# A fused gated-memory attention and MLP kernel on one core: a new hand-written issue order, with the last rows of w_in loaded behind q and k of steps 0 and 1

## The chip, the cores and the metric

The kernel runs on one NeuronCore of a Trainium2 chip. TensorE (PE) multiplies matrices into PSUM; VectorE (DVE), ScalarE (ACT) and GpSimd (POOL) work on what PE leaves there and on SBUF; SyncE (SP) issues all transfers from and to the chip's memory. Every engine takes its own instructions strictly in the order in which the program lists them and waits where one needs another engine's result. The metric is the time of one execution on the device in microseconds (us), median over runs; less is better.

## The reference

Two parts follow each other. The first is a recurrent attention with gates, for 4 batches and 8 heads over 768 positions with head size 40; the second is a two-layer MLP over the 3072 rows that it gives.

```python
for t in range(S):
    m_new = np.maximum(f_gate[:, :, t] + m, i_gate[:, :, t])
    f_stab = np.exp(f_gate[:, :, t] + m - m_new)
    i_stab = np.exp(i_gate[:, :, t] - m_new)
    m = m_new
    C = f_stab[..., None, None] * C + i_stab[..., None, None] * np.einsum('bhd,bhe->bhde', vt, kt)
    n = f_stab[..., None] * n + i_stab[..., None] * kt
    h_tilde = np.einsum('bhde,bhe->bhd', C, qt)
    denom = np.maximum(np.abs(np.einsum('bhd,bhd->bh', n, qt)[..., None]), 1.0)
    y[:, :, t] = o * h_tilde / denom          # o = sigmoid(o_gate)
x = y.transpose(0, 2, 1, 3).reshape(B * S, H * D)         # 3072 x 320
h = x @ w_in                                              # 320 x 2048
g = h * erf(np.maximum(h, 0.0) + np.log1p(np.exp(-np.abs(h))))
return g @ w_out                                          # 2048 x 320
```

## The kernel before, in words

**Attention.** The 768 positions are cut into 6 chunks of 128; with 4 batches that makes 24 steps s = 4c + b. `gate_chunk(c)` (line 369) scans the gates of a chunk for all batches at once (tokens gload, scan, sum, rest, split, at, atc, and cumw and decw, which write the running sums to DRAM to be read back in a broadcast form). `attention(s)` (line 446) does one step: load brings q and k (512 KB), loadv brings k, v and the output gate (484 KB); for the first four steps the decay matrix comes from PE (pe, two halves, lines 527 to 530) and ACT (ex), later from a broadcast read (bq), an add on POOL (add) and ex; sel masks it on POOL; S multiplies k and q (line 604, and 617 and 623 from chunk 1 on); w multiplies by the decay on DVE; ph gives the step's output (711, 718, 724); ab, rc, cl, yg, y and yy divide and gate it; tr (791) transposes it on PE; xh and xl split it into a rounded part and the rest for the MLP.

**Weights.** w_in and w_out are split likewise. w_in comes in four column parts p and two blocks k of 128 rows (`weights_in`, line 878, token win with p and k: win00, win01, win10, ...; 512 KB each), and its last 64 rows in two transfers of 256 KB to the two halves of the partitions (`weights_tail`, line 889, tokens tail0 for parts 0 and 1, tail1 for parts 2 and 3). val (ACT), dec (DVE), hi and lo decode them; for win00 to win11 the rest comes by PE (lp, lines 860 and 861). For the tail the tokens are valt, dect, hit and lot.

**MLP.** `mlp(f)` (line 980) is one of 24 phases. A phase has two halves g = 0, 1. In each, two up tokens (line 1031) multiply x by w_in into two PSUM banks, hb copies each bank to SBUF (ACT or DVE), sp (softplus) and er (erf) run on ACT, each with a table switch (line 258) unless the table stands, mu multiplies on DVE (1065), gh rounds (ACT or DVE), gl takes the rest (1076, DVE or POOL), and two dn tokens multiply by w_out (1111 to 1114). up f.0 and f.1 with dn f.0 and f.1 are the first half, up f.2 and f.3 with dn f.2 and f.3 the second. The first two phases keep g whole and have no gh and gl. o copies the sums out and st stores them.

**Order.** Nothing is scheduled when the program is built. `SEQUENCE` (line 155) is a list of tokens written by a search outside the kernel; `Plan.issue` (line 68) calls the parts in this order, so it is the program order of every engine's instructions and of SP's transfers:

```python
        for token in sequence:
            if token[0] == '+':
                for _ in range(int(token[1:])):
                    self.filler.fn()
            else:
                name, _, k = token.partition('.')
                found[name][int(k or 0)].fn()
```

A token +n issues n filler matmuls (line 333), which multiply constants into a bank that nobody reads; the token fill is one more. `ENGINES` (line 92) says for parts that two or three engines can do which one does them. `HOMES` (line 130) says for every buffer, in the order of issue, which place it gets: big are the 4 KB places in SBUF, bank six banks of PSUM, letters a to f. A new tile in a place waits until all readers of the old one are done.

In the list of before, S of step 1 stands ahead of S of step 0, and SP's transfers begin gload0, cst, win01, win10, gload1, loadv0, tail0, load1, loadv1, load0, load2, gload2, win00, loadv2.

Of the kernel before, what the change touches and what calls it, by code (L numbers as in the profile page):

```python
# [93 lines left out]
hb0.0 hb0.3 hb1.0 hb1.1 hb1.2 hb1.3 hb10.0 hb10.1 hb10.2 hb10.3 hb11.0 hb11.2 hb11.3 hb12.0 hb12.1 hb12.2  # L94
hb12.3 hb13.0 hb13.1 hb13.2 hb13.3 hb14.2 hb14.3 hb15.0 hb15.1 hb15.2 hb16.0 hb16.1 hb16.2 hb16.3 hb17.0
hb17.2 hb18.3 hb19.0 hb19.1 hb19.2 hb19.3 hb2.0 hb2.1 hb2.2 hb2.3 hb20.0 hb20.1 hb20.3 hb21.0 hb21.1 hb21.3
hb22.0 hb22.3 hb23.2 hb23.3 hb3.0 hb3.1 hb3.3 hb4.0 hb4.2 hb4.3 hb5.1 hb5.3 hb6.1 hb6.2 hb6.3 hb7.1 hb7.3
hb8.1 hb8.3 hb9.0 hb9.2 sk0.0 sk1.0 sk3.0
# [67 lines left out]
wout8 sel4 dn0.1 hio4 hio0 load5 dq4 ma4 bq7 dq5 valo8 hb1.3 hii21 deco8 sp1.1 wout6 ma5 hb1.0 hb1.1 sp1.0 er1.0
S5 w5.0 vg4 S4 mk4 na4 bq6 qa5 dn0.0 dn0.2 dq7 hio2 mk5 loi21 w4.1 w4.0 cumw2 qa4 add7 tail1 dn0.3 er1.1 ph4 na5
w5.1 ph5 mu1.0 win20 wout9 valo6 deco6 mu1.1 dq6 yg5 add6 o0.0 ab4 o0.1 th4 yg4 hio3 loo3 hio8 load6 ab5 loadv6
rc5 ma7 hio6 gexp2 loo6 loo8 dn1.0 cl5 valt1 load7 win31 rc4 decw2 cl4 y4 yy4 ex7 y5 rest3 ex6 dn1.1 dn1.3 yy5
dect1 hio1 tr4 valo9 deco9 xh4 xl4 at3 atc3 win30 tr5 xh5 xl5 hit3 dn1.2 loadv7 hit2 hio9 lpo9 nk4 nk5 bq8 up2.0  # L170
# [15 lines left out]
ab11 rc11 gl6.0 cl11 load13 y11 dn5.3 o5.1 up7.2 load14 dn6.1 ma12 w12.1 mk12 qa12.1 yy11 tr11 xh9 xl9 sp6.1
xh11 sp7.0 add13 dq13 hb7.2 xl11 xl10 ex13 sel13 dn6.0 ma13 up7.3 vg13 qa12.0 th12 up9.0 er6.1 mu6.1 gh6.1 hb7.3
hb9.0 th13 bq15 qz13 S13 ph12 ab12 w13.0 mk13 er7.0 mu7.0 rc12 cl12 gl6.1 rest4 cumw4 sp7.1 er7.1 add15 ex15
na13 na12 gh7.0 nk12 dq15 up9.2 w13.1 up8.2 qa13.0 add14 mu7.1 dn6.2 st4.0 yg12 y12 yy12 dn6.3 gexp4 loadv15
up10.2 dq14 hb8.2 nk13 hb9.2 gh7.1 up8.3 ex14 gl7.0 tr12 xh12 xl12 up8.0 th15 loadv14 dn7.1 qa13.1 sel15 th14  # L190
vz15 up10.0 gload5 qz14 scan5 hb10.2 ph13 sum5 hb8.0 qa14.1 sel14 vg14 load15 vz14 ma14 dn7.0 rest5 loadv17
gl7.1 S14 hb10.0 up10.1 qa14.0 w14.0 mk14 na14 nk14 up8.1 ab13 hb8.3 hb10.1 vg15 qz15 qa15.1 vz16 at5 w14.1 ma15
S15 dn7.2 atc5 mk15 up9.3 ph14 w15.1 rc13 cl13 sp8.1 hb8.1 yg13 qz19 qa15.0 w15.0 ph15 y13 hb9.3 sp8.0 yy13 tr13
er8.1 ab14 rc14 up10.3 na15 ab15 rc15 er8.0 at4 sp9.1 yg15 cl15 y15 decw4 o7.0 hb10.3 mu8.0 gh8.0 xh13 yy15
# [1025 lines left out]
```

## Time and profile before

| | us |
|---|---|
| median of 3 runs | 444.38 |
| the runs | 444.38, 444.69, 440.9 |
| the profiled execution | 444.52 |
| its span, from the first to the last instruction | 442.8 |
| PE busy in it | 435.2 |

The span is 1.7 us shorter than the time of the same execution. Times in rows count from the start of the span. In a row of the timeline a piece of neighbouring instructions is shown together, with the count behind the x; since matmuls overlap, the time from the start of one piece to the start of the next is what it costs PE. A waiting time in square brackets names who ended it.

### The profile page before, as it was taken

What the parts mean: (1) busy time and instruction counts of PE and PEld (TensorE: products, weight loads), DVE (VectorE), ACT (ScalarE), POOL (GpSimd) and SP (SyncE); (2) the same over time, 40 slices, a digit from 0 to 9 for tenths busy, and PEclk for the clock granted to TensorE, in tenths of its full rate; (3) what the DMA queues carried; (4) which work ended last, traced back from release to release, by engine and by line L of the source; (5) the groups of instructions that cost most, each with busy time, mean ns of one, the idle gap of its engine ahead of it and who ended that gap; (6) DMA issues with size and microseconds to landing.
All of it is one profiled execution on the core that took longest, in us unless ns stands there. A gap on an engine that the chain in (4) does not pass through costs nothing.

```text
span 442.8 us, 12907 instructions
## 1 busy us (share of the span) xinstructions
PE 435.2 (98%) x5404; PEld 386.2 (87%) x5404; DVE 328.4 (74%) x588; ACT 326.2 (74%) x423; POOL 171.9 (39%) x175
## 2 busy tenths in 40 slices
PE   8899999999999999999999999999999999999996
...
PEclk9789999999999999999999999999999999999999
...
GB/s 201 329 306 291 164 173 350 99 185 94 181 231 122 127 145 48 172 130 92 121 33 151 178 152 46 83 166 119 114 89 4 3 0 1 0 31 0 46 1 59
DMA packets 31373, 53.52 MB, mean 121 GB/s; under 512 B 4308, under 2 KB 19444, under 8 KB 31316
## 3 DMA queue, kind: packets, MB, share of 16 engines
q1 hardware_dynamic: 31316, 52.71, 39.1%
...
## 4 chain that ended last, share of the span: by engine, by line
PE 65%; DVE 1%; issue 1%; ACT 0%; ACTq 0%
PE h L1031 29%; PE po L1111 10%; PE po L1114 10%; PE po L1112 10%; PE pa L711 2%; PE pa L617 2%; PE pa L791 1%; PE pa L623 1%; DVE st L682 0%; DVE st L689 0%; DVE z L647 0%; DVE gl L1076 0%; DVE o L1124 0%; ACT o L279 0%; DVE z L633 0%
## 5 line engine op out<-in xcount | busy, mean ns | idle before, releaser
L1031 PE MATMUL h<-xx,wh 128*128 128x256 f32 (+1 forms) x768 | 180.7, 340 | 1.4 <-issue 1.2
L1031 PEld LDWEIGHTS h<-xx,wh 128*128 128x128 f32 x768 | 125.6, 188 | 16.2 <-issue 0.5
L1111 PE MATMUL po<-woh,gh 128*128 128x320 f32 x352 | 106.8, 312 | 0.0
L1112 PE MATMUL po<-wol,gh 128*128 128x320 f32 x352 | 105.5, 309 | 0.0
L258 ACT ACT_TABLE_LOAD x80 | 102.6, 1283 | 1.5
L1031 PE MATMUL h<-xx,wl 128*128 128x256 f32 (+1 forms) x256 | 86.3, 337 | 0.0
L1065 DVE TENSOR_TENSOR hb<-e,hb 128x1024 f32<-128x1024 f32 x44 | 57.6, 1321 | 36.9 <-ACT e L1057 36.7
L1114 PE MATMUL po<-woh,gl 128*128 128x320 f32 x352 | 76.4, 309 | 0.0
L1076 POOL TENSOR_TENSOR gl<-hb,gh 128x1024 fp32r<-128x1024 f32 x16 | 40.5, 2535 | 90.1 <-DVE gh L281 39.1
L279 ACT ACTIVATE hb<-h 128x512 f32<-128x512 f32 x68 | 39.5, 590 | 39.5 <-PE h L1031 31.8
L1111 PEld LDWEIGHTS po<-woh,gh 128*128 128x128 f32 x352 | 66.1, 188 | 1.2
L1112 PEld LDWEIGHTS po<-wol,gh 128*128 128x128 f32 x352 | 66.2, 188 | 0.7
L1114 PEld LDWEIGHTS po<-woh,gl 128*128 128x128 f32 x352 | 57.8, 188 | 0.1
L1031 PEld LDWEIGHTS h<-xx,wl 128*128 128x128 f32 x256 | 48.2, 188 | 7.2 <-issue 1.4
L1052 ACT ACTIVATE e<-hb 128x1024 f32<-128x1024 f32 x48 | 50.3, 1059 | 4.3 <-DVE hb L281 2.4
L1057 ACT ACTIVATE e<-e 128x1024 f32<-128x1024 f32 x48 | 50.2, 1057 | 0.4
L1076 DVE TENSOR_TENSOR gl<-hb,gh 128x1024 fp32r<-128x1024 f32 x28 | 38.6, 1381 | 6.0 <-ACT gh L279 3.3
L560 POOL TENSOR_TENSOR dm<-dm,aT 128x512 f32<-128x512 f32 x20 | 23.7, 1193 | 39.9 <-DMA dm<-cum_dr 26.6
L571 POOL TENSOR_SCALAR_AFFINE_SELECT dm<-dm 64x512 f32<-64x512 f32 x40 | 31.2, 780 | 18.4 <-ACT dm L565 16.8
L281 DVE COPY hb<-h 128x512 f32<-128x512 f32 x28 | 19.1, 686 | 21.6 <-PE h L1031 21.2
L633 DVE TENSOR_TENSOR z<-pa,dm 64x256 f32<-64x256 f32 x64 | 26.9, 420 | 6.2 <-PE pa L623 3.8
L647 POOL TENSOR_TENSOR z<-z,dq 40x512 f32<-40x512 f32 x16 | 22.5, 1409 | 18.6 <-DMA z<-in_qk_dram 8.1
...
## 6 DMA issues: line engine op xcount, KB each, us to landing
...
```

The costliest lines, as they stand in the source:

```text
L258: nc.add_instruction(mybir.InstLoadActFuncSet(name=nc.get_next_instruction_name(), engine=mybir.EngineType.Activation, act_func_set_id=loa ...
L279: nc.scalar.activation(to, of, AF.Copy)
L571: nc.gpsimd.affine_select(out=v.dm[r], in_=v.dm[r], pattern=[[0, H], [1, HL]], compare_op=ALU.is_ge, fill=0.0, base=0, channel_multiplier=-1)
L633: nc.vector.tensor_tensor(ofj(v.z[0:HL, :, r])[:, j], v.ps[j][r], ofj(v.dm[r])[:, j], op=ALU.mult)
L1031: nc.tensor.matmul(V.h[i][:, n * width:(n + 1) * width], w, m, start=q == 0 and not cut, stop=q == len(ops) - 1 and (not cut or n == len(m ...
L1052: nc.scalar.activation(V.e, V.hb, AF.Softplus)
L1057: nc.scalar.activation(V.e, V.e, AF.Erf)
L1065: nc.vector.tensor_tensor(V.g if full else V.hb, V.e, V.hb, op=ALU.mult)
L1076: engines[e].tensor_tensor(V.gl, V.hb, V.gh.bitcast(F32), op=ALU.subtract)
L1111: nc.tensor.matmul(po, V.gh[:, ts], woh[:, w], start=start, stop=False)
L1112: nc.tensor.matmul(po, V.gh[:, ts], wol[:, w], start=False, stop=False)
L1114: nc.tensor.matmul(po, V.gl[:, ts], woh[:, w], start=False, stop=stop)
```

## The change

Three things of the plan are replaced as a whole: `SEQUENCE`, `HOMES` for big, bank, bits, den and st, and `ENGINES`. No function changes. The same parts are issued, in another order, and some on another engine: 42 of the 96 copies hb on DVE (28 before), 54 on ACT (68); 17 gl on POOL (16), 20 qa on POOL (16), 18 vg on POOL (12), 12 y on DVE (6), 16 o on ACT (12), 12 xh on ACT (9), 20 hi on ACT (17). At the start 30 fillers stand in one row and 7 stand after S2 (before 7, 21 and 9). SP's transfers begin gload0, cst, win10, loadv1, win01, gload1, load0, loadv0, load1, tail0, gload2, win00, load2, loadv2. S of step 0 stands ahead of S of step 1, and of w_in's parts 01 and 10 the tokens lp stand behind S1 and ph1 and no longer ahead of S1. Shown are the first line of the banks, the start of the list, and the places of the later stretches that the prediction speaks of.

```diff
-abcdefcbedfbafedbfacbdfeabcdafecdfaecdfbcdaefcfcaefcadbefcafdbcdbeacbdfaeaedfcbabcadebfcabdedefbacddbeadbceadf
...
+abcdefbcabfdcbefdacedabecfbaecfbdcfabdcefbdacefcedafcbedafcebdafcebaedfcabadbfcaedafcbaedbafedfaedbebfdcabecfe
...
-small gload0 ident select scan0 sum0 +7 cst +21 minus mask ones win01 vali01 win10 vali10 rest0 split0 pe0.0
-pe2.0 deci01 hii01 gload1 scan1 sum1 pe1.0 ex1.0 deci10 pe2.1 loadv0 tail0 ex2.0 pe1.1 ex1.1 lpi01 fill valt0
-dect0 sel2.0 rest1 hii10 lpi10 hit0 ex2.1 load1 pe3.0 hit1 lot1 sel1.1 loi01 loadv1 ex3.0 sel1.0 S1 pe0.1 load0
-load2 ex0.0 ex0.1 S0 vg1 w1.0 gload2 w1.1 pe3.1 vg0 w0.0 win00 loadv2 w0.1 ph1 scan2 sum2 gexp1 ex3.1 loi10 ph0
-sk1 ab1 ab0 rc0 sk0 rest2 at1 atc1 vali00 sel2.1 vg2 lot0 rc1 load3 cl1 S2 +9 th2 th0 sel3.0 at2 cl0 deci00
-hii00 th1 yg0 w2.0 win11 vali11 y0 yy0 lpi00 yg1 w2.1 y1 deci11 tr0 loi00 atc2 cumw1 xh0 xl0 S3 yy1 tr1 xh1 ph2
-sel3.1 loadv3 xl1 wout2 hii11 lpi11 loi11 valo2 yg2 vg3 th3 w3.0 w3.1 deco2 wout4 ab2 bq4 add4 up0.0 hb0.0 valo4
-rc2 ph3 ab3 cl2 yg3 gload3 rc3 cl3 y2 yy2 up0.2 ex4 tr2 wout1 xh2 y3 bq5 up0.3 wout0 deco4 win21 loadv4 yy3 tr3
-valo1 scan3 hb0.2 xl2 loadv5 xh3 wout3 xl3 up0.1 sk3 hb0.1 valo0 deco0 hb0.3 up1.0 add5 ex5 sel5 decw1 deco1
...
-dn7.3 o7.1 st5.1 atc4 xl13 loadv16 sp10.0 er10.0 gl8.0 bq17 yg14 tr15 up9.1 up11.0 bq19 up11.2 cl14 y14 hb9.1
-load17 mu8.1 nk15 sp9.0 er9.0 vz19 cumw5 yy14 tr14 add17 ex17 gh8.1 dn8.0 gl8.1 dn8.2 mu9.0 mu10.0 xh14 dn8.1
-st5.0 sp10.1 xh15 xl15 er9.1 hb11.0 er10.1 gh9.0 gl9.0 th17 dn8.3 add19 up11.1 mu9.1 dn9.0 sel17 gh9.1 up11.3
-st7.0 gexp5 hb11.1 sp11.0 mu10.1 gh10.1 dq17 hb11.2 gl9.1 gh10.0 dn9.1 dn9.3 gl10.0 dn10.1 gl10.1 vg17 qz17
...
-sp17.0 ph22 ph23 yg22 gl16.1 ph21 up17.2 sp18.1 er18.1 yg23 ab22 rc22 hb19.0 ab21 xl20 rc21 cl22 y22 yy22 yg21
-dn16.0 dn16.2 hb17.2 tr22 cl21 up17.3 er17.0 mu17.0 mu18.1 xh22 y21 yy21 ab23 er18.0 mu18.0 gh17.0 tr21 up19.3
-hb17.3 sp17.1 up19.1 gl17.0 rc23 cl23 y23 yy23 dn17.0 er17.1 dn16.1 dn16.3 dn17.1 xh21 gh18.1 xl21 tr23 hb19.3
-mu17.1 gh17.1 gl17.1 dn17.2 dn17.3 gh18.0 gl18.0 dn18.0 xh23 sp19.1 er19.1 dn18.1 mu19.1 hb19.1 sp19.0 er19.0
...
-hb23.1 sp23.0 er23.0 mu23.0 gh23.0 gl22.1 dn22.2 dn22.3 st15.3 gl23.0 dn23.1 gl23.1 dn23.3 o23.2 st23.2 dn23.0
-dn23.2 o23.0 o23.1 o23.3 st23.3 st23.0 st23.1
...
+small select +30 gload0 cst ident scan0 sum0 rest0 split0 win10 loadv1 win01 ones vali01 gload1 scan1 sum1 mask
+pe2.0 deci01 pe1.0 load0 ex1.0 pe1.1 ex1.1 pe2.1 loadv0 vali10 deci10 minus pe3.0 ex2.0 load1 pe0.1 pe0.0 ex0.0
+ex0.1 ex2.1 hii01 hii10 gexp1 rest1 S0 S1 tail0 sel2.0 sel1.1 sel1.0 vg1 th0 gload2 ex3.0 lpi01 loi01 valt0 vg0
+w0.0 win00 w1.0 pe3.1 w1.1 fill ph1 w0.1 ab1 lpi10 load2 ph0 scan2 ex3.1 sk1 dect0 sum2 rest2 S2 sel3.0 yg0 +7
+vali00 deci00 ab0 rc0 cl0 loadv2 gexp2 sel2.1 vg2 w2.0 cumw1 w2.1 hit1 rc1 win11 hit0 lot0 y0 loi10 cl1 th1 yg1
+hii00 at1 load3 lpi00 y1 vali11 loi00 ph2 sk2 loadv3 bq4 bq5 yy0 tr0 xh0 atc1 at2 sk0 deci11 yy1 wout0 atc2 xl0
+tr1 xh1 xl1 hii11 S3 sel3.1 vg3 w3.0 w3.1 th2 th3 lpi11 loi11 ab2 add4 ex4 up0.0 lot1 wout2 gload3 wout4 ph3
+add5 ex5 ab3 rc2 yg2 cl2 y2 up0.2 valo2 wout1 rc3 cl3 yg3 yy2 loadv4 y3 valo4 yy3 deco2 tr3 xh3 xl3 deco4 loadv5
+decw1 hb0.2 tr2 up0.3 xh2 wout3 xl2 scan3 hb0.0 hb0.3 wout8 valo0 up0.1 hb0.1 sk3 valo1 sum3 deco0 deco1 sp0.1
...
+hb11.0 hb11.1 nk15 dq17 up9.1 at5 hb10.1 tr13 o7.1 xh15 xl15 qa17.0 dn8.0 yy14 tr14 gl8.1 hb9.1 sp9.0 er9.0 ma17
+mu9.0 gh9.0 gh10.1 atc5 er9.1 dn8.2 dn8.1 gl9.0 dn8.3 dn9.1 up11.3 mu9.1 add17 gh9.1 gl9.1 dn9.3 sp10.0 xh13
...
+tr21 dn16.0 dn16.3 cl22 er19.1 st15.0 yg23 cl23 y23 yy23 hb18.3 mu17.0 y22 tr23 xh23 gh17.0 mu18.0 gl17.0 up17.3
+sp18.1 dn16.2 xh21 xl21 hb19.1 up17.2 sp19.0 hb17.2 gh18.0 yy22 hb17.3 tr22 xh22 xl22 gl18.0 dn17.0 dn17.1 xl23
+sp17.1 er17.1 mu17.1 up20.2 gh17.1 gl17.1 up20.3 er18.1 dn17.2 dn18.0 er19.0 mu18.1 dn17.3 dn18.1 mu19.0 gh19.0
...
+er23.0 mu23.0 gh22.1 hb23.2 gh23.0 gl22.0 up23.3 hb23.3 gl22.1 gl23.0 dn21.3 sp23.1 er23.1 mu23.1 dn22.0 dn22.1
+dn22.2 dn23.0 dn22.3 o19.3 st19.3 gh23.1 gl23.1 st15.2 dn23.2 o23.0 dn23.1 dn23.3 st23.0 st19.2 o23.1 st23.1
+o23.2 o23.3 st23.2 st23.3
```

## Rows read from the trace of the kernel before

**Rows 1.** The page: busy time of each engine; PE's work and clock by slices.
```profile
PE 435.2 (98%) x5404; PEld 386.2 (87%) x5404; DVE 328.4 (74%) x588; ACT 326.2 (74%) x423; POOL 171.9 (39%) x175
...
PE   8899999999999999999999999999999999999996
...
PEclk9789999999999999999999999999999999999999
```

**Rows 2.** Windows of 10 us: busy of each engine, granted clock, DMA share, GB/s.
```profile
0.00:10.00 10.00, 8.89 (x30) 3.38 (x31) 6.33 (x23) 5.44 (x8) 1.79 (x8) 1.00 0.72 202
10.00:20.00 10.00, 8.85 (x66) 5.33 (x67) 5.96 (x13) 5.47 (x11) 1.81 (x3) 0.82 0.96 303
20.00:30.00 10.00, 10.00 (x241) 7.58 (x237) 6.68 (x21) 4.79 (x13) 4.97 (x7) 0.67 0.93 332
```

**Rows 3.** Waits of PE: us in total, times, longest.
```profile
PE h L1031 <- issue: 1.2, 1, 1.2
...
PE pa L791 <- issue: 0.5, 1, 0.5
```

**Rows 4.** Timeline of PE, 0 to 35 us: start, us, line, operation, count.
```profile
1.11 8.68 PE L333 MATMUL po<-warm 128*128 128x512 bf16 x28 [1.11 <-DVE m L327]
...
11.10 0.38 PE L530 MATMUL pa<-spl,early 32*128 32x128 bf16 x4
...
15.01 0.50 PE L861 MATMUL pa<-wh,minus 128*128 128x512 f32 x1 [1.15 <-ACT wh L279]
...
15.98 1.81 PE L604 MATMUL pa<-qk 40*128 40x128 f32 x16
...
19.23 2.08 PE L604 MATMUL pa<-qk 40*128 40x128 f32 x16
...
27.37 2.13 PE L333 MATMUL po<-warm 128*128 128x512 bf16 x9
29.45 1.02 PE L860 MATMUL pa<-bits,ident 128*128 128x512 f32 x2
...
30.95 1.16 PE L604 MATMUL pa<-qk 40*128 40x128 f32 x16
...
32.52 0.82 PE L718 MATMUL pa<-kvo,dm 128*32 128x41 f32 x64
...
33.57 1.13 PE L860 MATMUL pa<-bits,ident 128*128 128x512 f32 x2
...
34.77 0.40 PE L1031 MATMUL h<-xx,wh 128*128 128x256 f32 x2
```

**Rows 5.** Timeline of ACT, 5 to 16 us.
```profile
6.55 0.67 ACT L840 ACTIVATE bits<-raw 128x512 f32<-128x512 f32 x1 [1.80 <-DMA raw<-in_w_in_dram]
7.82 0.67 ACT L840 ACTIVATE bits<-raw 128x512 f32<-128x512 f32 x1 [0.60 <-DMA raw<-in_w_in_dram]
...
11.55 0.59 ACT L540 ACTIVATE dm<-h 128x512 f32<-128x512 f32 x1
...
13.78 0.66 ACT L904 ACTIVATE bits<-raw 128x512 f32<-128x512 f32 x1 [1.15 <-DMA raw<-in_w_in_dram]
```

**Rows 6.** Windows of 1 us around the landing of w_in's last rows.
```profile
12.00:13.00 1.00, 1.00 (x5) 0.50 (x4) 0.00 (x0) 0.63 (x2) 0.80 (x2) 1.00 0.94 217
14.00:15.00 1.00, 0.00 (x0) 0.00 (x0) 0.49 (x2) 1.00 (x3) 0.01 (x1) 1.00 1.04 416
```

**Rows 7.** Timelines near the end: PE's dn and last up, DVE's last gl.
```profile
411.03 0.30 PE L1111 MATMUL po<-woh,gh 128*128 128x320 f32 x1
...
421.57 0.62 PE L1031 MATMUL h<-xx,wh 128*128 128x512 f32 x2
...
423.44 0.31 PE L1111 MATMUL po<-woh,gh 128*128 128x320 f32 x1
...
430.34 1.23 DVE L1076 TENSOR_TENSOR gl<-hb,gh 128x1024 fp32r<-128x1024 f32 x1 [1.25 <-ACT gh L279]
```

**Rows 8.** Groups of instructions by line: count, busy, mean ns, idle before.
```profile
L1076 POOL TENSOR_TENSOR gl<-hb,gh 128x1024 fp32r<-128x1024 f32 x16 | 40.5, 2535 | 90.1 <-DVE gh L281 39.1 <-ACT gh L279 30.8 <-issue 11.9
```

More of the change, by code (lines that the diff above doesn't have):

```diff
@@ L93 @@
 ENGINES.update(dict.fromkeys("""
[L94 to L98, printed above, removed]
+hb0.0 hb0.2 hb1.0 hb1.1 hb1.2 hb1.3 hb10.1 hb10.2 hb10.3 hb11.3 hb12.0 hb12.2 hb12.3 hb13.0 hb13.2 hb13.3
@@ L99 @@
+hb15.1 hb15.3 hb16.1 hb16.3 hb17.0 hb17.2 hb19.1 hb2.0 hb2.1 hb2.3 hb20.3 hb21.0 hb21.3 hb22.0 hb23.1 hb23.2
+hb23.3 hb3.1 hb3.2 hb4.0 hb4.1 hb4.2 hb5.0 hb5.1 hb5.2 hb6.0 hb6.1 hb6.2 hb6.3 hb7.0 hb7.2 hb7.3 hb8.0 hb8.1
+hb9.0 hb9.1 hb9.2 hb9.3 sk1.0 sk2.0
 """.split(), 'ACT'))
 ENGINES.update(dict.fromkeys("""
-cl0.0 cl10.0 cl12.0 cl13.0 cl14.0 cl20.0 cl21.0 cl3.0 cl7.0 gh10.0 gh11.1 gh13.1 gh14.1 gh15.0 gh16.0 gh16.1
-gh17.1 gh19.0 gh19.1 gh2.1 gh20.0 gh21.0 gh22.0 gh3.0 gh4.0 gh4.1 gh6.1 gh8.0 gh8.1 gh9.0 hii21.0 hii30.0
@@ L111 @@
-vg6.0 vg8.0 vg9.0
+gl10.0 gl13.0 gl16.0 gl17.0 gl19.0 gl20.1 gl21.0 gl21.1 gl22.0 gl22.1 gl23.0 gl23.1 gl5.1 gl6.0 gl6.1 gl7.1
+gl8.1 loi20.0 loi21.0 loi31.0 loo1.0 loo3.0 loo7.0 loo8.0 lot0.0 lot3.0 qa10.0 qa11.0 qa11.1 qa12.0 qa12.1
+qa13.0 qa13.1 qa15.1 qa16.0 qa16.1 qa18.0 qa19.0 qa20.0 qa21.1 qa22.0 qa22.1 qa23.1 qa8.0 qa9.0 qa9.1 vg1.0
+vg10.0 vg11.0 vg12.0 vg13.0 vg14.0 vg15.0 vg16.0 vg17.0 vg18.0 vg19.0 vg20.0 vg21.0 vg23.0 vg3.0 vg4.0 vg5.0
+vg6.0
 """.split(), 'POOL'))
@@ L166 @@
[L166 to L170, printed above, removed]
@@ L186 @@
[L186 to L190, printed above, removed]
@@ L191 @@
[L191 to L194, printed above, removed]
-dn7.3 o7.1 st5.1 atc4 xl13 loadv16 sp10.0 er10.0 gl8.0 bq17 yg14 tr15 up9.1 up11.0 bq19 up11.2 cl14 y14 hb9.1
@@ new lines @@
+dn0.3 loo4 tail1 er1.0 mu1.0 wout9 valo6 ph4 o0.0 o0.1 loo8 er1.1 ph5 ab4 yg5 th4 deco6 win20 rc4 cl4 dn1.0
+mu1.1 ab5 rc5 hio6 loo6 valt1 dn1.1 cl5 y5 yg4 y4 yy5 loadv6 valo9 gexp3 dn1.3 th6 deco9 yy4 tr4 loadv10 dect1
+hit3 lot3 bq7 loo2 tr5 hio9 ex6 sel6 xh4 xh5 dq6 xl4 xl5 dn1.2 win30 loo0 nk4 hio1 lpo9 hit2 lot2 up2.2 vz9
+hb2.2 th7 loo9 add7 load6 dq7 vali30 o1.0 o1.1 vali20 deci20 vg6 ex7 ma6 up2.3 win31 hii20 loi20 hb2.3 up2.0
+hb2.0 deci30 S6 qa6 load7 w6.1 mk6 up2.1 wout5 w6.0 up3.2 hii30 up3.0 na6 nk6 vali31 deci31 sel7 vg7 S7 loi30
@@ new lines @@
+er7.0 hb7.2 vg13 w12.0 hb7.3 o5.1 loadv14 st5.1 dn6.1 sel14 ma12 up9.0 hb9.0 bq15 mk12 na12 mu7.0 S13 qa12.0
+ph12 mu6.1 gh6.1 w13.1 nk12 up10.2 gl6.1 ab12 up8.0 th12 vz14 yg12 qa13.0 dn6.3 w13.0 load15 rc12 mk13 cl12
+dn6.2 gh7.0 gl7.0 dn7.0 vg14 hb8.0 hb8.1 dq14 na13 nk13 dq15 add15 vz15 ma15 S14 ma14 sp7.1 er7.1 y12 yy12 mu7.1
+gh7.1 ph13 ab13 tr12 qz14 w14.0 mk14 na14 up8.2 hb8.2 up10.3 at4 dn7.1 ex15 loadv15 th14 qa15.0 xh12 yg13 sel15
+vg15 qa14.0 decw4 gload5 sp8.0 qa15.1 up8.3 loadv16 xl12 qa14.1 hb10.2 hb10.3 sp10.1 er10.1 nk14 gl7.1 w14.1
@@ new lines @@
+hb8.3 sp8.1 S15 scan5 sum5 mk15 th16 ph14 dn7.3 yg14 mu10.1 ab14 rc13 cl13 cumw5 y13 w15.1 bq19 w15.0 er8.0
+up9.2 rest5 atc4 hb9.2 up9.3 rc14 up10.0 mu8.0 gh8.0 gl8.0 ph15 ab15 yy13 up11.1 th15 er8.1 qz17 mu8.1 yg15
+hb9.3 sp9.1 dn7.2 hb10.0 o7.0 bq17 up11.0 rc15 cl15 y15 yy15 cl14 y14 up10.1 vz16 qz19 tr15 gh8.1 na15 vz17
+hb11.0 hb11.1 nk15 dq17 up9.1 at5 hb10.1 tr13 o7.1 xh15 xl15 qa17.0 dn8.0 yy14 tr14 gl8.1 hb9.1 sp9.0 er9.0 ma17
+mu9.0 gh9.0 gh10.1 atc5 er9.1 dn8.2 dn8.1 gl9.0 dn8.3 dn9.1 up11.3 mu9.1 add17 gh9.1 gl9.1 dn9.3 sp10.0 xh13
```

114 lines of the change are left out of this document (58 added, 56 removed).

## The prediction

> **What bounds the kernel now.** I read the head of the page first. PE is busy for 435.2 of 442.8 us, and its row of slices shows a 9 from the third slice to the last but one [rows 1]. So TensorE's own work sets the time, and a change of order can win only in three places: the 7.6 us in which PE is idle, the time that its clock is held back, and matmuls that fill time without being needed. The clock row drops in the second and third slice only. The windows put a size on it: granted 0.82 from 10 to 20 us and 0.67 from 20 to 30 us [rows 2], that is 10 x 0.18 + 10 x 0.33 = 5.1 us of full clock missing. At 1.2 GHz half of the time is missing, so TensorE stood at that level for 10.2 us. The waits of PE in the middle are two that no engine explains, 1.2 and 0.5 us [rows 3].
>
> The first 35 us of PE's timeline [rows 4] then tell how this start goes. 28 filler matmuls end at 9.8. The products of the first gates (pe) follow; six of them end at 11.48. Two remainders of w_in (lp) run, the second held up by 1.15 us of idleness before 15.01. S1 starts at 15.98, and from there PE has no visible gap until up0.0, the first matmul of the MLP, at 34.77, but most of this stretch runs at the low level: S0 takes 2.08 us at 19.23 where S3 takes 1.16 at 30.95. On ACT the decode of w_in's last rows (valt0) stands 1.15 us until they land, at 13.78 [rows 5].
>
> After 34.77 the kernel is a wall of matmuls. So my sum has two parts: when up0.0 starts, and what idle time the new order puts into the wall.
>
> **The change, part by part.** It changes no instruction of the computation. By counting tokens, both lists put the same kinds and numbers on PE ahead of up0.0: 38 fillers, eight pe, four S, three ph, four lp, two at, two tr. In the whole list ACT loses 14 copies hb to DVE, and 80 table switches become 79; counted with the mean durations of their groups, ACT loses some 6 us of work in all, DVE keeps its total and POOL gains some 11, all far under PE's, so I cost the swaps of engine at nothing. The matmuls cover them; where that cover is thin is priced below.
>
> *Start of S0.* 30 fillers now stand in one row: 1.11 + 30 x 0.31 = 10.3 [rows 4]. The pe products cost about 0.25 each (28 fillers to 9.8, six pe to 11.48, with the mask's in it), the first seven end near 12.1. S0 now comes before S1 and takes a bank that ex2.0 frees. ACT's queue ahead of that: vali01 waits for win01, now the third large transfer and not the first. Transfers of that size landed 1.27 us apart (6.55, 7.82) [rows 5], so it lands at about 9.0; vali01 and mask hold ACT till 10.6. ex1.0 follows its product at 10.8, then ex1.1, vali10, minus and ex2.0, five instructions of 0.3 to 0.67 [rows 5], end at 13.3. S0 starts at 13.3. PE is idle for 1.2 us before it, as in the old start before 15.01.
>
> *The last rows of w_in (tail0)* now go after q and k of steps 0 and 1 (load0, load1). While they were in flight the queues moved 217 GB/s, just after 416 [rows 6]. Up to load1 the new list moves 3.36 MB; 2.02 MB had moved by 10 us [rows 2], the rest at 416 lands at 13.2, at 217 at 16.2. I take 13.9, near the fast end, since the slow rate goes with the tail. S0 then ends at 14.5 and S1 goes on without a wait.
>
> The Trainium skill, page "DMA: Bandwidth & Descriptors", section "Rules for kernel authors", says that two transfers to disjoint halves of the partitions share the same engines and serialize, so splitting neither helps nor hurts beyond that. By it the tail is worth one 512 KB transfer, the slow stretch from 10 to 13 us belongs to the time and not to the tail, load1 lands at about 14.8, and the sum would be 0.3 us more. The rate of 217 against 416 speaks for the row.
>
> *From S0 to up0.0.* Full-clock prices from [rows 4]: S 1.16 (30.95), ph 1.05 (32.52 to 33.57), lp 1.2 (33.57 to 34.77), an lp with a tr 1.5 (29.45 to 30.95), so tr 0.3, nine fillers and an at 2.08 (27.37 to 29.45). The new list has from S0 on four S 4.64, three ph 3.15, two lp with tr 3.0, two more lp 2.4, one pe 0.25, eight fillers 1.7, two at 0.2: 15.4 us. That puts up0.0 at 28.7, plus half of the time at the low level. With none of it the chain beside PE is later: win00 lands near 18.3 behind the tail, its decode waits in ACT's and DVE's queues till 23.5, w2 till 25.5, then ph2, tr, S3 and lpi11 give 30.0. With 10.2 us low as before it is 33.8. Which one? In the old start the low level holds over S1, pe0.1, S0 and pe3.1, and the clock is full again soon after ph1 and ph0. In the new one two lp and ph1 come right behind S1. I take 7 us low, an estimate between the two: 28.7 + 3.5 = 32.2, that is 2.6 us earlier than 34.77. Ends: 1.0 us (or 0.3 by the page) and 4.8.
>
> *New idle time in the wall.* I counted PE's work between the last up of each half phase and the first dn that needs its gl, with up 1.87 (421.57 to 423.44), dn 1.76 (six from 411.03 to 421.57) [rows 7] and tr 0.3. The chain between them is shown entire at the end of the trace: up ends at 423.44, gl at 431.57 [rows 7], 8.1 us with the first table switch hidden behind hb on DVE; 8.9 where hb is on ACT, since its 0.6 comes first and its hand-over. The old list leaves 8.8 or more everywhere after the first half phase. The new one falls below twice:
> - up9.1 to dn9.1: at5, tr13, tr14 and four dn, 7.8, with hb9.1 on ACT: 1.1 us of waiting. In the old order 12.9 stood there.
> - up17.2 to dn17.2: tr22, two dn, two up, 7.6. Here ACT is at softplus already, so one switch goes, but xh22 stands in the queue: 8.1, so 0.5 us. In the old order 11.4.
>
> Behind each waiting dn stand all later matmuls. Bounds: 0, if ACT runs ahead, to 5.1 and 3.8, if the chain needs all that the old order gave it. I take the chain's own length, the nearest row. Two smaller ones: tr3 before up0.3 waits for y3 and yy3, about 0.4 (0 to 1); at the end the gl of six half phases stand on POOL at 2.54 each [rows 8] where the last one took 1.23 on DVE, and dn23.2 has 0.3 too little (0 to 1.3).
>
> *The unexplained idles*, 1.2 and 0.5: no row ties them to the order. I count half as gone, 0.85 (0 to 1.7).
>
> *Queues.* gload2 still waits on SP for rest1, now near 14, with win00 behind it; the queues are busy with the tail until 16.5, which hides that. Without this cover win00 and with it up0.0 would be 1 us later at full clock, and nothing with the clock low.
>
> *Sum.* -2.6 + 1.1 + 0.5 + 0.4 + 0.3 - 0.85 = -1.15 on the profiled execution's 444.52 us (span 442.8 and 1.7 around it), which is 0.14 above the median of 444.38. So 443.3.
>
> **Rivals.**
> - *The clock stays up.* For it: lp and ph come earlier, 30 fillers are unbroken. Against it: the idle stretch before S0 is as long, and the pe and S that ran low are the same. Then up0.0 at 30.0, new waits at their low end (1.0 in all) and both idles gone: 444.4 - 4.8 + 1.0 - 1.7 = 438.9.
> - *It does not do what it says.* S0 and S1 start early, but the low level lasts as long and the later list (win00, its decode) eats the rest: -1.0 + 2.3 = 445.7.
> - *Slower: the thin places.* At dn9.1 and dn17.2 the chain stands in loaded queues: ACT was busy 326.2 of 442.8 us [rows 1] and serves two half phases there. If both need what the old order gave, 5.1 + 3.8 in place of 1.6 us: 443.3 + 7.3 = 450.6. It decides against the change once the two waits together pass 2.7 us. Against it: an average of 74% leaves ACT room.
>
> **How the numbers follow.** Forecast 0.50 (own range 441 to 446), clock stays up 0.20, nothing gained 0.14, thin places 0.16. A measurement of this kernel can tell about 1% from no change, 4.4 us: below 439.9 lies the second case, 0.20; above 448.8 the last, 0.16; between them 0.64. The range 438.8 to 449.4 leaves out somewhat under half of each outer case.
>
> **What would show it.** S0 at about 13.3 and ahead of S1; up0.0 between 30 and 34; a granted clock in 10 to 30 us whose missing part is under 5.1; in PE's waits a po line released by DVE gl of about 1 us near 213 us of the span and one of 0.5 near 357; 79 table switches, 54 hb on ACT. I am wrong if up0.0 starts later than 34.8, if idle time of PE after it passes 4 us, or if a wait stands where I counted room.

## The result, and the profile after

The changed kernel takes 446.68 us (median of 9 runs, 445.98 to 450.04) against 444.11 us for the kernel before in the same comparison (9 runs, 438.6 to 445.84): a ratio of 1.0108, 95% interval 1.0063 to 1.0154. By the medians it is slower by 2.6 us; the ratio counts as slow, and leaves out, the two runs of before that lie over 1.5% above its fastest (445.68 and 445.84), and the means of the rest, 447.38 and 442.59, are 4.8 us apart. I had forecast 1.1 us in the other direction. The profiled execution takes 446.68 us with a span of 445.0 us.

The head of the page and the windows of the first 30 us, against [rows 1] and [rows 2]:

```profile
PE 436.4 (98%) x5404; PEld 385.8 (87%) x5404; DVE 335.8 (75%) x588; ACT 322.1 (72%) x417; POOL 186.1 (42%) x181
...
PEclk9799999999999999999999999999999999999999
```
```profile
10.00:20.00 10.00, 8.48 (x74) 5.55 (x72) 7.61 (x15) 6.42 (x15) 4.28 (x6) 0.83 0.86 284
20.00:30.00 10.00, 9.95 (x230) 5.69 (x228) 6.80 (x21) 5.69 (x13) 1.33 (x2) 0.83 0.94 317
```

In this execution the clock did better than before: 10 x 0.17 + 10 x 0.17 = 3.4 us of full clock are missing, where 5.1 us were. But it is one draw. The mean granted clock of a whole run is on record for each run: over the nine runs of the changed kernel it is 0.984 to 0.992, and 0.989 or lower in seven, so that 5.1 us are missing on average. In the 131 runs of the kernel before beside the later experiments and in its repeat (three executions of over 590 us left out) it is 3.6 us. And up0.0 gained nothing even here. These are the two first S, up0.0 and the last piece of TensorE's timeline, to be read against [rows 4]; the last line is the same last piece in the kernel before:

```profile
13.67 1.16 PE L604 MATMUL pa<-qk 40*128 40x128 f32 x16
16.35 1.95 PE L604 MATMUL pa<-qk 40*128 40x128 f32 x16 [1.52 <-DMA qk<-in_qk_dram]
...
34.76 0.39 PE L1031 MATMUL h<-xx,wh 128*128 128x256 f32 x2
...
441.14 0.46 PE L1114 MATMUL po<-woh,gl 128*128 128x320 f32 x2
```
```profile
438.97 0.46 PE L1114 MATMUL po<-woh,gl 128*128 128x320 f32 x2
```

up0.0 starts at 34.76 (before 34.77). From there to the end of the last matmul, which I call the wall, it takes 441.60 - 34.76 = 406.84 us, before 439.43 - 34.77 = 404.66. So all of the 2.2 us between the two profiled executions stand in the wall. The windows of the two walls, before and after (length, then TensorE's busy time):

```profile
34.77:439.43 404.66, 402.73 (x4953) 366.54 (x4951) 304.98 (x525) 308.49 (x388) 159.42 (x152) 1.00 0.36 108
```
```profile
34.76:441.60 406.84, 404.36 (x4953) 367.61 (x4951) 313.02 (x528) 302.61 (x377) 174.39 (x160) 1.00 0.37 107
```

TensorE's idle time in the wall grew from 1.9 to 2.5 us; the other 1.6 us stand in its busy time for the same 4953 matmuls. What they are no view shows. The waits of TensorE, against [rows 3]:

```profile
PE pa L604 <- DMA qk<-in_qk_dram: 1.5, 1, 1.5
PE po L333 <- DVE m L327: 1.1, 1, 1.1
PE po L1114 <- DVE gl L1076: 0.9, 1, 0.9
PE pa L617 <- DMA qk<-in_qk_dram: 0.7, 1, 0.7
PE pa L711 <- DVE z L633: 0.5, 2, 0.3
PE pa L791 <- DVE kvo L785: 0.2, 1, 0.2
```

The first two belong to the start. The two idles of before that no engine explains are gone, and four new lines stand in the wall: a gl at 117 us, z and kvo at 151 to 154 us, and a load of q and k at 234 us, 2.3 us in all. None of them is at one of the places that I had named.

### The profile page after: what moved, and what is told of

It reads as the page before. It is cut to its first block, busy times and chain, and to the rows that moved or that the text cites. A ratio compares the mean times of both kernels' runs of the same rounds, so it can differ in the third digit from the quotient of the medians.

```text
span 445.0 us, 12901 instructions
## 1 busy us (share of the span) xinstructions
PE 436.4 (98%) x5404; PEld 385.8 (87%) x5404; DVE 335.8 (75%) x588; ACT 322.1 (72%) x417; POOL 186.1 (42%) x181
## 4 chain that ended last, share of the span: by engine, by line
PE 61%; DMA 2%; DVE 1%; ACT 1%; issue 0%; SPq 0%; ACTq 0%; DVEq 0%
PE h L1031 28%; PE po L1111 9%; PE po L1114 9%; PE po L1112 9%; PE pa L711 2%; PE pa L617 2%; PE pa L791 1%; DMA qk<-in_qk_dram 1%; PE pa L623 1%; DVE hb L1065 1%; DMA out_dram<-o 1%; ACT L258 0%; ACT e L1057 0%; ACT e L1052 0%; SPq L556 0%
## 5 line engine op out<-in xcount | busy, mean ns | idle before, releaser
L1031 PEld LDWEIGHTS h<-xx,wh 128*128 128x128 f32 x768 | 125.8, 188 | 15.4 <-issue 0.5
L1065 DVE TENSOR_TENSOR hb<-e,hb 128x1024 f32<-128x1024 f32 x44 | 56.5, 1293 | 25.8 <-ACT e L1057 25.6
L1076 POOL TENSOR_TENSOR gl<-hb,gh 128x1024 fp32r<-128x1024 f32 x17 | 43.1, 2536 | 75.6 <-DVE gh L281 36.7
L279 ACT ACTIVATE hb<-h 128x512 f32<-128x512 f32 x54 | 30.9, 592 | 41.5 <-PE h L1031 39.4
L281 DVE COPY hb<-h 128x512 f32<-128x512 f32 x42 | 28.5, 684 | 28.4 <-PE h L1031 28.0
L571 POOL TENSOR_SCALAR_AFFINE_SELECT dm<-dm 64x512 f32<-64x512 f32 x40 | 32.2, 806 | 41.5 <-ACT dm L565 40.0
L1076 DVE TENSOR_TENSOR gl<-hb,gh 128x1024 fp32r<-128x1024 f32 x27 | 34.5, 1284 | 4.3 <-ACT gh L279 2.0
L647 POOL TENSOR_TENSOR z<-z,dq 40x512 f32<-40x512 f32 x20 | 29.5, 1486 | 18.0 <-DMA z<-in_qk_dram 10.6
L279 ACT ACTIVATE gh<-hb 128x1024 fp32r<-128x1024 f32 x22 | 23.0, 1053 | 13.7 <-DVE hb L1065 12.1
```

The source lines that it names most:

```text
L279: nc.scalar.activation(to, of, AF.Copy)
L571: nc.gpsimd.affine_select(out=v.dm[r], in_=v.dm[r], pattern=[[0, H], [1, HL]], compare_op=ALU.is_ge, fill=0.0, base=0, channel_multiplier=-1)
L647: engines[e].tensor_tensor(v.z[64:QR, :, r], v.z[64:QR, :, r], v.dq[64:QR, :, r], op=ALU.mult)
L1031: nc.tensor.matmul(V.h[i][:, n * width:(n + 1) * width], w, m, start=q == 0 and not cut, stop=q == len(ops) - 1 and (not cut or n == len(m ...
L1065: nc.vector.tensor_tensor(V.g if full else V.hb, V.e, V.hb, op=ALU.mult)
L1076: engines[e].tensor_tensor(V.gl, V.hb, V.gh.bitcast(F32), op=ALU.subtract)
```

## The experiments

Walls are measured as above, in one profiled execution of each kernel, so that each is a single draw. The ratios are to the kernel before, run beside each kernel; its median there is given too. A ratio is not the quotient of the two medians, for the reason given with the result.

| kernel | median | before beside it | ratio, 95% interval | up0.0 | wall |
|---|---|---|---|---|---|
| before (as shown ahead) | 444.38 | | | 34.77 | 404.66 |
| before again | 442.49 | 443.13 | 1.0008, 0.9970 to 1.0046 | 32.15 | 403.43 |
| new start, old rest | 443.12 | 443.13 | 1.0003, 0.9968 to 1.0038 | 34.73 | 403.53 |
| old start, new rest | 447.34 | 443.13 | 1.0073, 1.0025 to 1.0120 | 34.46 | 407.55 |
| old, tail late | 443.89 | 443.13 | 1.0037, 1.0002 to 1.0072 | 34.60 | 403.34 |
| new, tail later | 446.87 | 442.07 | 1.0086, 1.0053 to 1.0119 | 35.84 | 407.54 |
| new, three mends | 443.87 | 442.07 | 1.0041, 1.0008 to 1.0075 | 33.18 | 404.99 |
| new, four mends | 445.75 | 442.93 | 1.0074, 1.0036 to 1.0112 | 33.63 | 404.62 |
| new, five mends | 444.29 | 443.82 | 1.0036, 1.0001 to 1.0072 | 36.98 | 403.22 |
| old without nine fillers | 443.14 | 442.07 | 0.9988, 0.9941 to 1.0036 | 33.66 | 402.29 |
| old, nine fillers ahead | 441.01 | 442.07 | 0.9976, 0.9939 to 1.0013 | 32.55 | 406.34 |
| the same again | 442.85 | 443.82 | 0.9990, 0.9949 to 1.0032 | 31.91 | 403.63 |
| old, 15 fillers ahead | 443.44 | 442.93 | 1.0030, 0.9994 to 1.0067 | 35.23 | 404.39 |
| old, early decode | 445.13 | 442.93 | 1.0071, 1.0030 to 1.0111 | 38.08 | 402.59 |

### Which half of the list loses?

Each hybrid takes one list up to up0.0 and issues what is left in the other's order, with the other's engines and places (the letters renamed at the seam so that the tiles alive there keep their places):

```python
start = A[:A.index('up0.0')]
sequence = start + [t for t in B if t[0] != '+' and t not in start]
```

New start, old rest: 

> The new list up to up0.0, then the old list's order, engines and places for the rest. Theory (the wall lost the time, the start gained nothing): up0.0 near 34.8 us, last matmul 404.7 us later, 444 to 445 us, ratio 1.000. Rival (the start of the new list carries the loss, by the clock or by what it leaves behind in the queues): 446 to 447 us, ratio 1.006, with up0.0 later or the wall longer than 406 us.

Old start, new rest: 

> The old list up to up0.0, then the new list's order, engines and places. Theory (the wall lost the time): up0.0 near 34.8 us, last matmul 406.8 us later, 446 to 447 us, ratio 1.006, and the waits at 115 us (gl on po) and at 233 us (a load of q and k) are there again. Rival (the start lost it): 444 to 445 us, ratio 1.000, and those waits are gone.

The theory holds in both, in ratio and wall. Only the new rest brings the waits of the wall, nearly as long as in the changed kernel:

```profile
PE po L1114 <- DVE gl L1076: 0.9, 1, 0.9
PE h L1031 <- issue: 0.7, 1, 0.7
PE pa L617 <- DMA qk<-in_qk_dram: 0.7, 1, 0.7
PE pa L711 <- DVE z L633: 0.6, 2, 0.4
```

So the rest of the list costs 0.73% or some 3.2 us, and the new start costs or brings nothing that can be told from none.

### What the waits of the wall are

*At 117 us.* gl3.1 is late on VectorE, and dn3.2 needs it. dn3.1, which needs only gl3.0, stands behind:

```profile
111.31 2.10 DVE L1076 TENSOR_TENSOR gl<-hb,gh 128x1024 fp32r<-128x1024 f32 x1 [0.52 <-ACT gh L279]
...
115.54 1.46 DVE L1076 TENSOR_TENSOR gl<-hb,gh 128x1024 fp32r<-128x1024 f32 x1
...
117.05 0.85 PE L1114 MATMUL po<-woh,gl 128*128 128x320 f32 x4 [0.88 <-DVE gl L1076]
```

*At 151 us.* ph11 needs both w11, which stand on VectorE behind y9. That takes 1.55 us and is needed only by tr9, behind ph11 and ph10:

```profile
148.33 1.55 DVE L779 TENSOR_TENSOR kvo<-kvo,den 128x320 f32<-128x320 f32 x1
...
150.61 1.78 DVE L633 TENSOR_TENSOR z<-pa,dm 64x256 f32<-64x256 f32 x4
...
151.28 0.97 PE L711 MATMUL pa<-st,z 104*32 104x41 f32 x12 [0.32 <-DVE z L633]
```

*At 234 us.* SyncE's queue stands still from 214.66 to 224.61, because loadv17 and bq16 wait for places in big. The store st7.0 is behind them, and load17 takes the place that st7.0 must first have read:

```profile
214.22 0.44 SPq L492 DMA_DIRECT2D dq<-dec_dr  x1
224.61 0.36 SPq L480 DMA_DIRECT2D kvo<-in_kvo_dram  x1
225.35 1.10 SPq L556 DMA_DIRECT2D dm<-cum_dr  x2
226.50 1.05 SPq L1140 DMA_DIRECT2D out_dram<-o  x2
230.24 0.35 SPq L472 DMA_DIRECT2D qk<-in_qk_dram  x1
```

The load lands 3.84 us later by the chain, and S17 waits for it. Three mends, nothing else changed:

```diff
-dn3.0 dn3.2 dn3.1 ma8
+dn3.0 dn3.1 dn3.2 ma8
...
-cl9 y9 mk11 w11.0 hb6.1 w11.1 gh5.0 up6.2
+cl9 mk11 w11.0 hb6.1 w11.1 gh5.0 y9 yy9 gl5.0 up6.2
...
-ex17 sel17 loadv17 vg17 bq16 gh10.0 add16 ex16 st7.1 gl10.0 hb11.2 dn9.0 hb11.3 st7.0
+ex17 sel17 st7.0 st7.1 loadv17 vg17 bq16 gh10.0 add16 ex16 gl10.0 hb11.2 dn9.0 hb11.3
```

> The new list with three places of its wall changed and nothing else: dn3.1 ahead of dn3.2 (it waits for no gl that comes late); VectorE's mk11 and both w11 ahead of y9, with yy9 and gl5.0 behind y9; the stores st7.0 and st7.1 ahead of loadv17 on SP's queue, where they stood behind a bq that waits for its place. Theory (these three waits are the loss): the waits at 115, 151 to 154 and 233 us go, 3.9 us in all, the wall falls from 406.8 to 403.0 us, 442.5 to 443.5 us, ratio 1.000. Rival (each wait had a second one right behind it, since the same queues serve the next step): the wall stays above 405.5 us, 445 us or more, with new waits within 10 us of the old ones.

All three are gone from the waits, and both theories were half right: 1.85 us of the wall came back (TensorE's list shows 2.3 us for these waits, not 3.9), and new idle time stands at 158 us.

```profile
PE pa L791 <- DVE st L689: 1.0, 1, 1.0
PE pa L791 <- DVE den L771: 0.3, 1, 0.3
```

The fourth mend gives cl11, yy11, y10 and yy10 to VectorE (in `ENGINES`; they had been on GpSimd). (404.5 in the next text is 404.99 without the last piece's own 0.46.)

> The new list with the three mends and a fourth: cl11, yy11, y10 and yy10 on VectorE, where they stood on GpSimd behind gl5.1 and sel12 (the mended kernel waited 0.45 and 1.25 us for tr11 and tr10 near 158 us, while VectorE stood idle for 3.6 us). Theory (the wall of the new list loses only by such waits): these two waits go as well, the wall falls from 404.5 to some 403, the old list's length, 442 to 442.5 us, ratio 1.000. Rival (the next wait takes over once more): a new wait of 1 us or more after 155 us, wall above 404, ratio 1.004.

The rival won: the wait for den is gone, a wait of 1.1 us is left, and the wall is 404.62. Its name, st of L689, was the clue: nk11 on VectorE is the last reader of the bank that tr10 takes.

```diff
-ab10 rest4 dn5.1
+ab10 rest4 na11 nk11 dn5.1
...
-yy10 na11 nk11 sel13
+yy10 sel13
```

> The new list with the four mends and a fifth: VectorE's na11 and nk11 right behind rest4. With four mends tr10 still waited 1.13 us, named st of nk11: the bank that tr10 takes is read last by nk11, which stands behind the y10 that was moved to VectorE. Theory (a wait on a place, at the tail of a queue): it falls below 0.5 us, the wall from 404.6 to 403.6 us, which is the old list's length (403.4 to 404.7), ratio 1.000 to 1.003 by the start's luck. Rival (the new wall has losses of its own beside the visible waits): wall at 404.4 or more although no wait above 0.5 us is left in it, ratio 1.005 or above.

No wait of the wall is left in the list of TensorE's waits, only the two of the start:

```profile
PE pa L604 <- ACT x L420: 1.8, 1, 1.8
PE po L333 <- DVE m L327: 1.1, 1, 1.1
```

The wall is 403.22 us, within the old list's (402.29 to 404.66, but for one profile with a long stop, told below), with 0.13 us of idle time and 403.09 us busy:

```profile
36.98:440.20 403.22, 403.09 (x4953) 367.35 (x4951) 309.54 (x532) 302.00 (x377) 173.98 (x156) 1.00 0.37 107
```

So the mended places were the loss of the wall, with most of the part that the list of waits does not show: the busy time is 0.4 us over that of before, and the two idles of before are not there. With one profile of each, the step of the first three mends is clear of the spread of the old walls; those of the fourth and the fifth lie about within it.

The time, 1.0036, keeps the sign of a loss; this profiled execution had a late start (up0.0 at 36.98). The recorded clocks say where the sign comes from. Of the runs that enter the ratios, those with a mean clock of 0.990 or lower have a median of 447.2 us in the changed kernel (7 runs), 444.8 with five mends (8) and 444.5 in the kernel before (26). At one clock the loss is gone, as far as so few runs can tell; the kernel with five mends has this low clock in 8 of its 12 runs.

### The last rows of w_in alone

The old list, with tail0 behind load0 and its decode further behind:

```diff
-loadv0 tail0 ex2.0 ... valt0 dect0 sel2.0 ... hit0 ex2.1 load1
+loadv0 ex2.0 ... sel2.0 ... ex2.1 load1
...
-load0 load2
+load0 tail0 load2
```

> The old list with one part of the change: the last rows of w_in (tail0) load behind q and k of steps 1 and 0, and their decode (valt0, dect0, hit0, hit1, lot1) stands behind the last ex and sk of the start. Theory (the start is TensorE's work in order plus its wait for the tail's decode and load1): lpi10 starts near 13 us and not 15.0, S1 near 13.8 and not 16.0, up0.0 near 32.5, wall as before, 442 to 443 us, ratio 0.995. Rival (the later list, win00 and its decode, or a longer low clock eats it): up0.0 at 34.3 or later, 444 to 445 us, ratio 1.000.

The first half came as expected: lpi10 goes through without its wait and S1 starts at 13.71. Then the gain is given back in one place:

```profile
18.25 0.59 PE L718 MATMUL pa<-kvo,dm 128*32 128x41 f32 x15
21.11 0.85 PE L718 MATMUL pa<-kvo,dm 128*32 128x41 f32 x49 [2.27 <-issue]
```

ph0 stops after 15 of its matmuls and waits for nothing that the profile shows. Behind this idle the clock is low (0.66 from 20 to 30 us), and up0.0 is at 34.60.

In the changed kernel, tail0 was in flight beside load1. Moved behind gload2 (`vg1 th0 gload2 tail0`):

> The new list with tail0 behind gload2 on SP's queue, so that it is issued near 15 us and not at 7.5 us, beside load1. Theory (load1 landed at 16.2 and not 13.9 because the last rows of w_in were in flight beside it): TensorE's wait for load1 ahead of S1 (1.5 us) goes, S1 starts near 14.9, up0.0 near 33.3, 445 us, ratio 1.007. Rival (the queues were simply full, at some 300 GB/s in 10 to 20 us whatever is in them): the wait stays at 1 us or more and up0.0 at 34.5 or later, 446.7 us.

S1 now follows S0 without a gap, 32 matmuls in one row, so the tail beside it was what kept load1. But the same idle comes, longer, and the clock, at 1.00 from 14 to 23.4, is at 0.50 from 24 to 30 us:

```profile
13.89 2.40 PE L604 MATMUL pa<-qk 40*128 40x128 f32 x32
...
20.70 0.35 PE L718 MATMUL pa<-kvo,dm 128*32 128x41 f32 x14
23.45 0.83 PE L718 MATMUL pa<-kvo,dm 128*32 128x41 f32 x49 [2.40 <-issue]
```
```profile
14.00:23.40 9.40, 6.80 (x153) 4.63 (x154) 7.33 (x17) 6.10 (x14) 4.02 (x6) 1.00 0.71 215
24.00:30.00 6.00, 5.67 (x73) 3.80 (x64) 4.40 (x11) 2.99 (x7) 2.37 (x4) 0.50 0.91 328
```

### The idle without a reason, and the clock

> The kernel before, once more, to see what its spread (438.6 to 445.84 us) goes with. Theory: the granted clock at the start, so that runs under 442 us show a mean clock of 0.992 or more and those at 445 one of 0.988 or less. Rival: the clock is the same in short and long runs, and the spread comes from idle time of TensorE that differs from run to run (the two waits that no engine explains, 1.7 us in the profiled execution).

The profiled execution took 440.66 us with a clock of 1.00 in all of the first 40 us. So the clock is part of the spread, and the recorded clocks bear the theory out in the main: of the 107 runs of the kernel before that enter the ratios, the 27 with a mean clock of 0.998 or more took 438.0 to 441.2 us (median 440.2), the 26 at 0.990 or lower 442.0 to 445.7 (444.5). That is 4.3 us. In this profile only 2.6 of the 5.1 us of clock came back at up0.0, since ph0 stopped here too, at the very same matmul:

```profile
20.16 0.59 PE L718 MATMUL pa<-kvo,dm 128*32 128x41 f32 x15
22.50 0.67 PE L718 MATMUL pa<-kvo,dm 128*32 128x41 f32 x49 [1.75 <-issue]
...
32.15 0.40 PE L1031 MATMUL h<-xx,wh 128*128 128x256 f32 x2
```

The place counts in instructions. That points to their fetch, so I shifted the count: the nine fillers of the old list from behind S2 to ahead of ph1.

> The old list with the nine fillers ahead of ph1 and not behind S2. Theory (at full clock TensorE runs out of fetched instructions 15 matmuls into ph0, 1.7 to 2.5 us in three profiles, and fillers ahead of that give the fetch time): no wait on issue above 0.5 us in the start, and in full-clock starts up0.0 below 32, 441.5 us, ratio 0.997. Rival (the fetch is asked for only where the fetched instructions end): the wait is there again, 1.5 us or more, and the time stays, ratio 1.000 or above.

```profile
22.28 0.28 PE L718 MATMUL pa<-kvo,dm 128*32 128x41 f32 x6
23.14 0.73 PE L718 MATMUL pa<-kvo,dm 128*32 128x41 f32 x57 [0.59 <-issue]
```

Nine fillers more, and the stop comes after 6 matmuls of ph0 instead of 15: nine fewer. It sits at a fixed count, and it is shorter, since the fillers gave time. The page has a queue of its own for instructions, 42 packets; in the kernel with the tail late one of them stands inside the idle stretch, in the window from 18.8 to 19.9 us:

```profile
q1 hardware_dynamic: 124, 0.43, 97.3%
q8 instruction: 1, 0.02, 6.1%
```

No semaphore ties the two, so that the fetch is what TensorE waits for is inferred. But the traces of all kernels tie them by count and by time. Count TensorE's matmuls and weight loads together: the sixteen stops on issue of 0.48 us or more stand behind 447 to 449 of them (six profiles), 1215 to 1217 (five, near 42 us), 1983 (one, at 64.8 us) and 7871 to 7873 (four, at 262 to 266 us). But for the few records that a trace lacks, the distances are multiples of 256: 3 x 256, 6 x 256 and 29 x 256. And each of the sixteen ends 1.2 to 1.5 us behind the end of a packet of the instruction queue; of the shorter stops some do not. The two idles of before that no engine explained, 0.5 us behind 1217 and 1.2 us behind 7873, are among them. For the longer one the packet of the window from 263.6 to 264.7 us ends at 264.62:

```profile
266.07 0.39 PE L1031 MATMUL h<-xx,wh 128*128 128x512 f32 x1 [1.20 <-issue]
```
```profile
q8 instruction: 1, 0.02, 5.2%
```

In time the move came out at 0.9976, and again:

> The old list with the nine fillers ahead of ph1, once more on another occasion, since it came out at 441.01 us against 442.07 (0.9976, not separated from 1). Theory (it gives the fetch of instructions time where the clock is full, and costs nothing where it is low): ratio 0.995 to 0.999. Rival (the gain was the draw of the runs): 1.000 or above.

It came out at 0.9990: no gain that can be told from none, although its profile lists no stop in ph0 at all (the packet ended at 21.08, and TensorE passed the place at 22.52). In the first of the two, another such stop of 2.37 us stood in the wall at 64.8 us, which is why its wall is 406.34. Three more kernels with the old start:

> The old list without the nine fillers behind S2 (they feed nobody). Theory (TensorE's work in order sets up0.0): up0.0 is 2.1 us earlier than with them at the same clock, 441 us, ratio 0.995. Rival (a chain beside TensorE sets it: w_in's part 00 and its decode, then lpi00): TensorE waits ahead of lpi00 for ACT or VectorE some 2 us and up0.0 stays within 0.5 us, ratio 1.000.

up0.0 is at 33.66, with a stop of 1.91 us in ph0 and the clock at 0.67 from 20 to 30 us; ahead of lpi00 there is no wait. Whether the fillers cost anything is not settled, since the clock differs between the profiles.

> The old list with the nine fillers ahead of ph1 and six more ahead of lpi10, where TensorE stands idle for 1.5 us until ACT has decoded w_in's part 10. Theory (the idle stretch there is what lets the granted clock fall near 16 us, as in the profiled execution of before): the idle stretch shrinks below 0.6 us, the clock is 1.00 from 10 to 20 us, the runs near 445 us that the kernel before shows in half of its executions become rare, median 440.5 us, ratio 0.995. Rival (the clock falls wherever TensorE waits for instructions too, and is not decided there): the runs still fall in two groups, near 440.5 and near 444.5, ratio 0.998 or above.

The idle stretch ahead of lpi10's second matmul only shrank to 1.03 us, and in the profiled execution the clock fell all the same (0.87 from 10 to 20 us, 0.79 from 20 to 30 us). Over the runs the clock did hold more often: 0.995 or more in 10 of 12, and in 19 of 24 with the nine fillers alone, against 26 of 86 runs of the kernel before beside these three. What fell is the gain: at 0.998 or more the median is 442.6 us with 15 fillers and 440.5 with nine, where the kernel before has 440.2.

> The same list with the fillers, and the decode of w_in's part 00 (vali00, deci00, hii00) ahead of ab1 and sum2, lpi00 right behind S2, sel3.0 behind yy0. Theory (at full clock the chain win00, decode, lpi00, tr0, S3 sets up0.0, TensorE having waited 1.2 us ahead of lpi00): lpi00 starts near 25.6 and not 27.0, up0.0 near 31 and not 32.5, 439 us, ratio 0.993. Rival (y0 and S3 or the low clock set it): up0.0 within 0.5 us of the list without the early decode, the same time as that list.

lpi00 started early, at 26.75, but tr0 then waited 2.7 us for y0 on GpSimd, and up0.0 came at 38.08. No kernel here is faster than the one before by more than its interval.

## Why the prediction was wrong

Two parts of the sum failed. The start was to bring 2.6 us and brought none: the tail beside load1 had no price, the work was longer, and in most runs the clock was lower than I took it. The wall was to lose 1.45 us (2.3 of new waits less 0.85) and lost 2.2, at places that I had not looked at.

**The start of S0** (13.3) was nearly right, 13.67, in part by luck. TensorE did not stand idle ahead of it, where I had 1.2 us. The two pe of step 0 cost 0.86 us each with their mask and filled that time; I had priced all pe alike at 0.25.

**load1** failed. I took 13.9, near the fast end, "since the slow rate goes with the tail", and so let the tail come without a price although it was issued right behind load1. It shares the queues with it: S1 waited for load1 until 16.35, the slow end, and without the tail beside it there is no wait. That the slow end came out is luck: by windows of 1 us the queues moved 389 to 412 GB/s from 10 to 13 us, and then 246, 156 and 30. That is 1.64 MB by 16 us, about what was left up to the end of the tail (3.36 MB up to load1 and 0.52 for the tail, less 2.22 moved by 10 us). In the four other profiles of this start S1 begins at 14.97, 15.28, 16.27 and 16.93. The page of the Trainium skill that I weighed, "DMA: Bandwidth & Descriptors", section "Rules for kernel authors", gave 14.8 by its rule; all five measurements are later than both. Whether the two halves of the tail take turns is not shown here.

**From S0 to up0.0** I had 15.4 us of work at full clock and 3.5 us for the low level. The clock took 3.4 us. The wait for load1 took 1.5, and what is left is 34.76 - 13.67 - 3.4 - 1.5 = 16.2 us of work. So -2.6 became 0: load1 1.5, the start of S0 0.4, the work 0.8. That the clock took what I had forecast is the draw of this profile: over the nine runs it took 5.1 us on average. The new start itself goes with a low clock: in the five kernels that have it unchanged, 35 of 57 runs have a mean clock of 0.990 or lower and 3 one of 0.998 or more, in the kernel before 48 and 27 of 131. Why is not shown. I also took the work in order plus the clock for the bound, and no part of the sum allowed for the stop in the fetch that comes where the clock is full. It does not explain this result, since no profile of the unchanged new start has such a stop of 0.5 us or more before up0.0, but with the tail later, at full clock, it took 2.4 us. In the other profiles with the new start unchanged, up0.0 came at 34.73, 33.18, 33.63 and 36.98, and never at 32.2.

**The wall.** My +1.1 and +0.5 stood at dn9.1 and dn17.2. Neither waited, and no wait is listed for the two smaller terms (+0.4 and +0.3). At the first, up9.1 ended at 216.66 and gl9.0 at 224.2:

```profile
220.83 1.23 DVE L1065 TENSOR_TENSOR hb<-e,hb 128x1024 f32<-128x1024 f32 x1 [1.59 <-ACT e L1057]
222.17 0.69 DVE L281 CAST gh<-hb 128x1024 fp32r<-128x1024 f32 x1
...
222.96 1.23 DVE L1076 TENSOR_TENSOR gl<-hb,gh 128x1024 fp32r<-128x1024 f32 x1
```

That is 7.5 us, not the 8.9 that I took from the end of the trace, and it fits into the 7.8 of work. The step that failed here is the search itself: I looked only at the distance from up to dn and took every instruction of the chain as ready to run. The waits that came are a gl behind two w (the slack of dn3.2 counted, but VectorE's queue was full), a w behind a y, and a load behind a store behind a load: positions in VectorE's and SyncE's queues. Five mends of positions, engines and one bank's reader took the wall from 406.84 to 403.22. I had named SyncE's queue only for the start. The swaps of engine that I costed at nothing were hardly tested: the fourth mend undoes two of them (y10, yy10) together with two other moves, and the wall changed by 0.37 us. VectorE's busy time, which I had unchanged, rose from 328.4 to 335.8 us.

**The unexplained idles** I priced at half gone, with the remark that no row ties them to the order. They went wholly in the profiled execution, 1.7 us and not 0.85. By the count told above both are stops of the fetch, so the order has a say in them: it sets which instructions stand at the counts where they come. For the longer one the runs agree: 229 us behind up0.0 it is there again in the second profile of before (1.1 us), with the new start and the old rest (0.9 us) and with 15 fillers (0.7 us), in none of the profiles with the new rest, though not in every one with the old rest.

**Rivals.** "It does not do what it says" (445.7, chance 0.14) came closest: the start gave nothing and the wall lost 2.2 us, for which I had 2.3, but at other places, so that the number is luck. "The clock stays up" fell (no clock above 0.992 in nine runs), and so did "the thin places": the loss is of its size class but at other places, by another mechanism.
